# Attention, dense layer and soft mixture of experts in one kernel: the first batch's reduction of v moved behind the first pair's weights, and three loads of w_in moved ahead of five loads of v

## The chip, the core and the metric

The kernel runs on one core of a Trainium2 chip. The metric is the device time of one execution in microseconds. Before the change three executions took 735.56, 733.87 and 732.2 us, a median of 733.87 us. One further execution, 740.27 us long, was profiled; every row below comes from that one.

## What is computed

Three layers follow one another, on 4 batches of 12 heads, 448 positions and 64 columns per head:

```python
scores = scale * np.matmul(q, k.transpose(0, 1, 3, 2))      # masked above the diagonal
attn = softmax(scores);  x = np.matmul(attn, v)             # -> (1792, 768)
h = x @ w_in;  g = np.maximum(0.01 * h, h);  x = g @ w_out  # w_in (768, 2048), float64 in memory
logits = x @ phi                                            # soft mixture of experts, 8 experts of 4 slots
slot_input = softmax(logits, axis=0).T @ x
out = softmax(logits, axis=1) @ (relu(slot_input @ w1) @ w2)
```

## The kernel before, in words

Attention goes pair by pair: 24 pairs of two heads, six to a batch. A pair is written as three slots (`attention_slots`). For pair n they hold, in this order: `attend(n-1)`, the product of the previous pair's weights with its v (PSUM tile O); `lowering(n)`, which transposes the row maxima of pair n on TensorE (mps) and copies them to mr on ScalarE; three calls of `maxima(n+1, ...)`, whose scores (S_3, then S_0 with row blocks 0 and 2, then S_1) VectorE reduces into mxe by the line L361 (junk); three calls of `weights(n, g)` (T_0, T_1, T_2), each ended by an exponential on ScalarE (L397) and, for the last two, by a selection (L401) and sums (L406, L410) on GpSimd; `inverses` and `columns` of the pair before, with a reciprocal on VectorE (L438) and the scaling of O by s_v (L458); and at the end `qk_stacks(n+2)`, four plus four transposes (qkps), with the loads for later pairs behind them.

`reduce_v(n)` takes the largest absolute value of one pair's v on VectorE (L324). With the sixth pair of a batch it also reduces the six numbers (L327) and calls `pow2_scale`, which spreads the result over the partitions by a small matmul (L111, tile v_ps) and works out a power of two from it in five small VectorE instructions (L113 to L121): s_v, used first in `columns`, and inv_v. Before the loop the kernel before calls `reduce_v` for all six pairs of batch 0.

Between the slots, units of w_in are converted from float64: `load_raw` loads a unit of 768 KB (raw_i), ScalarE takes the absolute value (L196) and the sign (L197), VectorE the largest (L199), a shift (L200) and a merge (L201), a small matmul (w_ps) and the same small instructions give the scale (L113 to L121), ScalarE multiplies the sign by it (L215), GpSimd multiplies the two (L216) and splits the product (L220, L223). Six units belong to the first stage, the six pairs of batch 0, with three buffers for the raw data.

The order on each engine is set by a scheduler with the program's order as a start; the matmuls called through `mm` and `tr` keep the order in which they are written (`in_order`), while those called as `nc.tensor.matmul` may be placed by the scheduler. Every load is issued from SyncE (SP) in the order of the code. Once set, each engine carries out its own list strictly in order.

After the first stage the 16 column groups of w_in times x (PSUM tile H) are interleaved with the attention of the next batch, then come the units of w_out, the logits, and in the end the experts, whose weights (w) are loaded while they are used.

Of the kernel before, what the change touches and what calls it, by code (L numbers as in the profile page):

```python
# [29 lines left out]
def as_float(bits):  # L30
    return struct.unpack("<f", struct.pack("<I", bits))[0]
# [3 lines left out]
def tile_attn_moe_softmoe(ctx: ExitStack, tc: tile.TileContext, q, k, v, w_in, w_out, phi, w1, w2, out, dbg=None):  # L35
    nc = tc.nc
# [10 lines left out]
    NP = H // 2  # L47
# [10 lines left out]
    ident = const.tile([128, 128], F32, name="ident")  # L58
# [30 lines left out]
    def ps_tr(name, shape=(128, 512)):  # L89
        return psum.tile(list(shape), F32, tag="tr", bufs=TR[0], name=name)  # L90
# [12 lines left out]
    mm = partial(in_order, nc.tensor.matmul)  # L103
# [3 lines left out]
    def pow2_scale(absmax, name, shift=23, bias=0, out=None):  # L107


        ps = ps_tr(f"{name}_ps", (128, 128))  # L110
        nc.tensor.matmul(ps, absmax.to_broadcast([128, 128]), ident, start=True, stop=True)  # L111
        m1 = const.tile([128, 1], F32, tag="p2_m1", bufs=2, name=f"{name}_m1")
        nc.vector.tensor_reduce(m1, ps, AX.X, ALU.max)  # L113
        nc.vector.tensor_scalar(m1, m1, as_float((27 + bias) << shift), None, ALU.max)
        e = const.tile([128, 1], I32, tag="p2_e", bufs=2, name=f"{name}_e")
        nc.vector.tensor_scalar(e, m1.bitcast(I32), shift, None, ALU.logical_shift_right)
        si = const.tile([128, 2], I32, tag="p2_s" + name[0], bufs=4, name=f"{name}_s")
        nc.vector.tensor_scalar(si[:, 0:1], e, -(2**23), (268 + bias) * 2**23, ALU.mult, ALU.add)
        if out is None:
            out = si[:, 1:2].bitcast(F32)  # L120
        nc.vector.tensor_scalar(out.bitcast(I32), e, 2**23, -(14 + bias) * 2**23, ALU.mult, ALU.add)  # L121
        return si.bitcast(F32)[:, 0:1], out
# [31 lines left out]
    def load_raw():  # L154

        while waiting:
            u = waiting[0]
            kind, f, h, stage = u
            pool, n = pools[stage], BUFS[stage][0]
            if pool is None or sum(x[3] == stage for x in raws) == n:  # L160
                return
            waiting.pop(0)
            w = DM if h is None else DH
            t = pool.tile([128, w, 2], I32, tag="raw", bufs=n, name=f"raw_{kind}{f}_{h}")
            with tc.issue_after(last_load[0]):
                if kind == "i":
                    nc.sync.dma_start(
                        t.rearrange("p (c f) t -> p c (f t)", f=128),
                        w_in32[:, 256 * f : 256 * (f + 1)].rearrange("(c p) f -> p c f", p=128),
                    )  # L170
                else:
                    c0 = 2 * w * (h or 0)
                    nc.sync.dma_start(
                        t.rearrange("p c t -> p (c t)"), w_out32[128 * f : 128 * (f + 1), c0 : c0 + 2 * w]
                    )
            raws[u] = t
# [3 lines left out]
    def loaded_last():  # L180
        last_load[0] = next(
            i for i in reversed(nc.cur_bb.bb.instructions[-80:]) if i.engine == mybir.EngineType.SP
        )
# [112 lines left out]
    def load_qk(n):  # L296
        b, hp = divmod(n, NP)
        t = att.tile([CP, 2, 2 * NI * D], F32, tag="qk", bufs=2, name=f"qk{n}")
        t = t.rearrange("p j (c x) -> p j c x", c=NI)
        for j, src in enumerate((q, k)):  # L300
            for a in range(2):
                nc.sync.dma_start(
                    t[:, j, :, D * a : D * (a + 1)], src[b, 2 * hp + a].rearrange("(c p) d -> p c d", p=CP)
                )
        qk_t[n] = t
        loaded_last()

    def load_v(n):
        b, hp = divmod(n, NP)
        t = vring.tile([CP, 2 * NI, D], F32, tag="v", bufs=VRING, name=f"v{n}")  # L310
        nc.sync.dma_start(t, v[b, 2 * hp : 2 * hp + 2].rearrange("h (j p) d -> p (h j) d", p=CP))
        v_t[n] = t
        loaded_last()
# [4 lines left out]
    def reduce_v(n):  # L318

        b, hp = divmod(n, NP)  # L320
        if hp == 0:
            v_am[b] = am = const.tile([128, NP + 1], F32, tag="v_am", bufs=2, name=f"v_am{b}")
            nc.vector.memset(am, 0.0)
        nc.vector.tensor_reduce(v_am[b][:CP, hp : hp + 1], v_t[n], AX.XY, ALU.max, apply_absolute_value=True)  # L324
        if hp == NP - 1:
            am = v_am[b]
            nc.vector.tensor_reduce(am[:, NP:], am[:, :NP], AX.X, ALU.max)  # L327
            s_v[b], inv_v[b] = pow2_scale(am[:, NP:], f"v{b}")

    def qk_stacks(n):  # L330

        t = qk_t.pop(n)
        st = att.tile([128, 2, 2, S], F32R, tag="qs", bufs=2, name=f"qkt{n}")
        for j in range(2):
            p = ps_tr(f"qkps{n}_{j}", (128, S))
            for c in range(NI):
                tr(p[:, CP * c : CP * (c + 1)], t[:, j, c], ident[:CP, :CP])
            nc.scalar.copy(st[:, j, 0], p)  # L338
            nc.vector.tensor_tensor(st[:, j, 1], p, st[:, j, 0].bitcast(F32), ALU.subtract)  # L339
        st_t[n] = st  # L340

    def maxima(n, tiles):

        st = st_t[n]
        ps = psum.tile([CP, 2, 512], F32, tag="S", bufs=2, name=f"S{n}_{tiles[0]}")
        at = 0
        for i in tiles:
            w = CP * (i + 1)
            for a in range(2):
                r = slice(64 * a, 64 * a + 64)  # L350
                mm(
                    ps[:, a, at : at + w], st[r, 0, 0, CP * i : w], st[r, 1, 0, :w], start=True, stop=True,
                    skip_group_check=True,
                )
            at += w
        at = 0
        for i in tiles:
            w = CP * (i + 1)
            for a in range(2):
                junk = att.tile([CP, S], BF16, tag="junk", bufs=1, name=f"junk{n}_{i}_{a}")  # L360
                nc.vector.tensor_tensor_reduce(  # L361
                    out=junk[:, :w], in0=ps[:, a, at : at + w], in1=mask[:, S - w :], scale=-1.0, scalar=3e38,
                    op0=ALU.add, op1=ALU.min, accum_out=mxe[n % 2][:, 64 * a + i : 64 * a + i + 1],
                )
            at += w
# [126 lines left out]
    def attention_slots():  # L492


        for n in range(2):
            qk_stacks(n)
            load_qk(n + 2)
            if n == 0:
                for tiles in TILES:
                    maxima(0, tiles)  # L500
        for x in range(NP):
            reduce_v(x)
        for n in range(NPAIR + 1):
            here, more = n < NPAIR, n + 1 < NPAIR
            if n > 0:
                attend(n - 1)
            if here:
                lowering(n)
            if more:
                maxima(n + 1, TILES[0])  # L510
            if here:
                weights(n, 0)
            yield
            if n > 0:
                inverses(n - 1)
            if more:
                maxima(n + 1, TILES[1])
            if here:
                weights(n, 1)
            yield  # L520
            if n > 0:
                columns(n - 1)
            if here:
                weights(n, 2)
            if more:
                maxima(n + 1, TILES[2])
            if n + 2 < NPAIR:
                qk_stacks(n + 2)
                if n + 4 < NPAIR:
                    load_qk(n + 4)  # L530
            if n + NP < NPAIR:
                load_v(n + NP)
            if NP <= n + NP - 1 < NPAIR:
                reduce_v(n + NP - 1)
            yield

    TILES = ((3,), (0, 2), (1,))
    slots_of_attention = attention_slots()


# [208 lines left out]
    if True:  # L749
        pools[0] = tc.alloc_tile_pool(name="conv1", bufs=1)  # L750
        load_qk(0)
        load_qk(1)
        for n in range(NP):
            load_v(n)
        load_raw()
        nc.sync.dma_start(phi_sb, phi.rearrange("(c p) s -> p c s", p=128))
        stage(SLOTS * NP + LEAD, EARLY[0])
        tc_release(pools[0])
# [96 lines left out]
        for c in range(4):  # L855
            wo = loaded.pop(("wo", c))
            for h in range(2):
                for t in range(4):
                    nc.tensor.matmul(
                        psi[h][32 * t : 32 * t + 32], gdt[:, t, c], wo[:, t, 384 * h : 384 * (h + 1)],  # L860
                        start=c == 0, stop=c == 3, skip_group_check=True,
# [17 lines left out]
        for e in range(E):  # L879
            ph = ps2(f"ph{e}", (128, 256), tag="h", bufs=4)  # L880
            for hf in range(2):
                wt = loaded.pop(("w1", (e, hf)))
                for t in range(3):
                    for g in range(4):
                        nc.tensor.matmul(  # L885
                            ph[32 * g : 32 * g + 32], sit[:, 3 * hf + t], wt[:, t, 256 * g : 256 * (g + 1)],
                            start=hf == 0 and t == 0, stop=hf == 1 and t == 2, skip_group_check=True,
# [69 lines left out]
        for x, (t0, nt, c0, cols) in enumerate(pieces):  # L957
# [4 lines left out]
            for h in (0, 1) if cols == DM else (c0 // DH,):  # L962
                for t in range(nt):
# [3 lines left out]
                        start=t0 + t < 4, stop=t0 + t >= 8 * E - 4, skip_group_check=True,  # L967
# [52 lines left out]
```

## Time and profile before

| what | value |
|---|---|
| median of three executions | 733.87 us (732.2 to 735.56) |
| profiled execution | 740.27 us, of which 738.5 us are the span of the profile |
| busy share of the span: PE, DVE, ACT, POOL | 87%, 47%, 41%, 31% |
| shares of the chain that ended last: PE, DMA, ACT, DVE, POOL | 59%, 15%, 8%, 7%, 4% |

PE is TensorE, DVE is VectorE, ACT is ScalarE, POOL is GpSimd, SP is SyncE. Times in rows are microseconds from the start of the span. "L324" is line 324 of the kernel. In a timeline row the number in brackets is how long the engine had been idle, and what ended it. Instructions on one engine overlap a little at their ends, so the distance from one start to the next is what an instruction costs in a row of busy ones; it is up to 0.1 us less than the duration shown. The whole change is in the first 45 us of the program, so nearly all rows come from there.

### The profile page before, as it was taken

The page shows a single profiled execution, that of the slowest core. Times are in us where ns is not written, and L with a number is a line of the kernel's source. Part 1 is how long each engine was busy: PE and PEld are TensorE (multiplying, and loading weights), DVE is VectorE, ACT ScalarE, POOL GpSimd, SP SyncE. Part 2 cuts the span into 40 slices and gives each one's busy share as a digit, 9 for nine tenths or more (in the row PEclk, how much of TensorE's full clock was granted, in tenths as well). Part 3 has the DMA queues.
Part 4 walks back from the last instruction along what each step waited for, and adds up shares of the span by engine and source line. Part 5 has one row for each costly group of instructions (what it writes and reads, how often), then busy time and mean ns, then how long its engine had stood idle before and what let it go on. Part 6 is the DMA issues. An engine that isn't in the chain of part 4 may idle for free.

```text
span 738.5 us, 13147 instructions
## 1 busy us (share of the span) xinstructions
PE 639.2 (87%) x5196; PEld 372.0 (50%) x5196; DVE 344.6 (47%) x923; ACT 305.9 (41%) x615; POOL 228.9 (31%) x247
## 2 busy tenths in 40 slices
PE   3888769999898999899999989999999997984573
PEld 2555445555555556566555555664656543541122
DVE  5887655666864544453354544324444433110013
ACT  1777543756774455444345454422322220110013
POOL 4577832656873332441223332320000000000000
PEclk9999968999999999899999999999999999999867
DMA  9933263455544454421153222014859247999988
GB/s 195 249 81 76 62 186 93 122 145 148 152 145 157 124 174 141 136 93 51 51 145 90 66 65 66 22 51 171 300 224 338 87 172 297 409 399 401 392 276 261
DMA packets 117709, 125.73 MB, mean 170 GB/s; under 512 B 69520, under 2 KB 99216, under 8 KB 117648
## 3 DMA queue, kind: packets, MB, share of 16 engines
q1 hardware_dynamic: 117648, 124.90, 52.6%
q8 instruction: 41, 0.67, 0.4%
q14 instruction: 20, 0.16, 0.1%
HBM read 105.74 MB, written 19.14 MB: 169 GB/s over the span
## 4 chain that ended last, share of the span: by engine, by line
PE 59%; DMA 15%; ACT 8%; DVE 7%; POOL 4%; issue 4%; SPq 2%; DVEq 0%; ACTq 0%; POOLq 0%
PE H L100 25%; DMA w<-in_moe_w_dram 7%; PE O L100 7%; PE gps L100 4%; PE T L100 4%; DMA v<-in_v_dram 3%; PE pg L100 2%; PE ph L885 2%; PE L L100 2%; DMA raw_i_None<-in_moe_w_in_dram 2%; PE qkps L100 2%; ACT mr L373 2%; PE dn L100 2%; PE rb L100 2%; DMA raw_o<-in_moe_w_out_dram 2%
## 5 line engine op out<-in xcount | busy, mean ns | idle before, releaser
L100 PE MATMUL H<-x,w 128*128 128x448 f16 x1152 | 244.4, 358 | 6.0 <-DVE g L615 6.0
L100 PEld LDWEIGHTS <-w 128*128 128x128 f16 x1152 | 110.1, 99 | 110.4 <-issue 29.7
L361 DVE CUSTOM_DVE_ANT_0 junk<-S,mask 112x448 bf16<-112x448 f32 (+1 forms) x192 | 84.9, 442 | 36.0 <-PE S L100 32.7
L615 DVE SCALAR_TENSOR_TENSOR g<-H,iv,g 128x448 f32<-128x448 f32 x58 | 39.6, 683 | 98.4 <-ACT g L614 96.0
L614 ACT ACTIVATE g<-H,iv 128x448 f32<-128x448 f32 x58 | 36.6, 631 | 81.2 <-PE H L100 70.9
L397 ACT ACTIVATE P<-T 112x672 f32<-112x672 f32 (+1 forms) x72 | 56.8, 788 | 32.3 <-PE T L100 32.3
L100 PE MATMUL O<-P,v 112*64 112x448 f32 (+3 forms) x384 | 59.2, 453 | 5.8 <-POOL P L401 4.6
L100 PE MATMUL T<-qkt 64*112 64x336 f32 (+3 forms) x576 | 58.7, 315 | 5.2 <-ACT P L397 4.5
L401 POOL TENSOR_SCALAR_AFFINE_SELECT P<-P 112x448 f32<-112x448 f32 x48 | 29.4, 613 | 99.9 <-ACT P L397 99.9
L965 PE MATMUL po<-w,hz 128*32 128x384 f32 x256 | 30.8, 608 | 24.9 <-DMA w<-in_moe_w_dram 24.9
L100 PEld LDWEIGHTS T<-qkt 64*112 64x112 f32 x576 | 44.8, 183 | 11.5 <-ACT P L397 5.8
L100 PEld LDWEIGHTS O<-P,v 112*64 112x64 f32 x384 | 27.9, 151 | 36.6 <-issue 16.9
L373 ACT ACTIVATE mr<-mps,own 128x112 fp32r<-128x112 f32 x96 | 26.1, 355 | 45.4 <-PE mps L100 45.4
L410 POOL TENSOR_TENSOR tsum<-tsum,P 112x448 f32<-112x448 f32 (+1 forms) x48 | 43.9, 915 | 2.7
L406 POOL TENSOR_TENSOR tsum<-P 112x672 f32<-112x672 f32 x24 | 40.7, 1694 | 1.7
L554 ACT COPY g_nat<-gps 112x512 f32<-112x512 f32 x32 | 18.7, 584 | 53.5 <-PE gps L100 53.5
L556 DVE COPY g_nat<-gps 112x512 f32<-112x512 f32 x32 | 22.1, 692 | 37.8 <-PE gps L100 37.5
L460 POOL TENSOR_TENSOR x<-rs,x 128x448 f16<-128x448 f32 x24 | 25.3, 1054 | 46.1 <-ACT x L459 46.1
L339 DVE TENSOR_TENSOR qkt<-qkps,qkt 128x448 fp32r<-128x448 f32 x48 | 28.3, 620 | 21.9 <-ACT qkt L338 21.8
L216 POOL TENSOR_TENSOR cv_i_None<-cv_i_None,cs_i_None 128x768 f32<-128x768 f32 x16 | 26.8, 1682 | 34.1 <-ACT cs_i_None L215 34.0
L100 PE MATMUL S<-qkt 64*112 64x448 f32 (+1 forms) x192 | 33.2, 387 | 3.6 <-DVE mxe L361 2.8
L100 PE MATMUL T<-mr,onesr 64*112 64x448 f32 (+1 forms) x192 | 32.1, 331 | 4.2 <-ACT mr L373 4.2
(178 smaller groups left out, 936.5 us busy)
## 6 DMA issues: line engine op xcount, KB each, us to landing
w<-in_moe_w_dram SPq DMA_DIRECT2D x32, 1536.0 KB, 18.2
raw_i_None<-in_moe_w_in_dram SPq DMA_DIRECT2D x16, 768.0 KB, 6.0
raw_o_None<-in_moe_w_out_dram SPq DMA_DIRECT2D x10, 768.0 KB, 5.1
g_far<-g SPq DMA_DIRECT2D x32, 224.0 KB, 2.0
gb<-g_far SPq DMA_DIRECT2D x8, 896.0 KB, 7.7
wo<-wsc SPq DMA_DIRECT2D x4, 1536.0 KB, 6.8
qk<-in_q_dram SPq DMA_DIRECT2D x48, 112.0 KB, 2.8
qk<-in_k_dram SPq DMA_DIRECT2D x48, 112.0 KB, 2.8
```

The costliest lines, as they stand in the source:

```text
L100: op(*args, **kwargs)
L216: nc.gpsimd.tensor_tensor(t, t, sg, ALU.mult)
L339: nc.vector.tensor_tensor(st[:, j, 1], p, st[:, j, 0].bitcast(F32), ALU.subtract)
L361: nc.vector.tensor_tensor_reduce(out=junk[:, :w], in0=ps[:, a, at : at + w], in1=mask[:, S - w :], scale=-1.0, scalar=3e38, op0=ALU.add, o ...
L373: nc.scalar.activation(mr[:, i], ps, AF.Copy, scale=own[:, i : i + 1])
L397: nc.scalar.activation(x[:, :, o : o + at], ps[:, :, :at], AF.Exp, scale=SCALE)
L401: nc.gpsimd.affine_select(out=d, in_=d, compare_op=ALU.is_ge, fill=0.0, base=0, pattern=[[0, 4], [1, CP]], channel_multiplier=-1,)
L406: nc.gpsimd.tensor_tensor(tsum[:CP], p[0][:CP, :, 0, CP:], p[0][:CP, :, 1, : S - CP], ALU.add)
L410: nc.gpsimd.tensor_tensor(y, y, p[1][:CP, :, j, : S - CP * (j + 2)], ALU.add)
L614: nc.scalar.activation(g, ps, AF.Copy, scale=iv[b][:, 0, f : f + 1])
L615: nc.vector.scalar_tensor_tensor(g, ps, iv[b][:, 1, f : f + 1], g, ALU.mult, ALU.max)
L965: nc.tensor.matmul(po[h][32 * g : 32 * g + 32], hp[:, (t0 + t) % 8], wt[:, t, DH * h - c0 : DH * (h + 1) - c0], start=t0 + t < 4, stop=t0 ...
```

## The change

Three edits. The small matmul of `pow2_scale` for batch 0 goes through `mm`, which binds it to its place in the written order of TensorE. The reductions of v of batch 0 move from ahead of the pair loop into it: pairs 0 to 4 ahead of `attend(0)`, and the sixth, with the power of two, behind `weights(1, 0)`. And the first three units of w_in are asked for behind v of pair 0 and ahead of v of pairs 1 to 5.

```diff
-        nc.tensor.matmul(ps, absmax.to_broadcast([128, 128]), ident, start=True, stop=True)
+        (mm if name == "v0" else nc.tensor.matmul)(ps, absmax.to_broadcast([128, 128]), ident, start=True, stop=True)
@@ attention_slots
-        for x in range(NP):
-            reduce_v(x)
         for n in range(NPAIR + 1):
             here, more = n < NPAIR, n + 1 < NPAIR
+            if n == 1:
+                for x in range(NP - 1):
+                    reduce_v(x)
             if n > 0:
                 attend(n - 1)
...
                 weights(n, 0)
             yield
+            if n == 1:
+                reduce_v(NP - 1)
             if n > 0:
                 inverses(n - 1)
@@ the loads at the start
         load_qk(0)
         load_qk(1)
-        for n in range(NP):
+        load_v(0)
+        load_raw()
+        for n in range(1, NP):
             load_v(n)
-        load_raw()
```

On TensorE, before the change, the matmul v_ps of batch 0's largest v stands between the transposes of q and k of pair 1 (qkps) and the transposed maxima of pair 0 (mps):

```order
L100 MATMUL qkps_1_242<-ident,qk_163 128x112 x4
L111 MATMUL v_ps<-ident,v_am_254 128x128
L100 MATMUL mps_273<-ident,mxe_143 128x112
L100 MATMUL S_3_280<-qkt_234 112x448 x2
L100 MATMUL T_0_287<-qkt_187 112x448 x6
L100 MATMUL T_0_287<-mr_275,onesr 112x448 x2
```

After the change the same place on TensorE reads:

```order
L100 MATMUL qkps_1_242<-ident,qk_163 128x112 x4
L100 MATMUL mps_254<-ident,mxe_143 128x112
L100 MATMUL S_3_261<-qkt_234 112x448 x2
L100 MATMUL T_0_268<-qkt_187 112x448 x6
L111 MATMUL w_ps<-ident,w_am_278 128x128
L100 MATMUL T_0_268<-mr_256,onesr 112x448 x2
```

v_ps is gone from here (it now stands behind T_0 of pair 1), and the matmul w_ps of the first unit of w_in, which stood behind S_0 of pair 1, has moved up into T_0.

On ScalarE the copies (CAST) of the transposed q and k of pair 1 (qkt_234) now have the first unit of w_in between them. This is the place after the change; before it, the two copies stood next to each other:

```order
L338 CAST qkt_234<-qkps_0_235 128x448
L196 ACTIVATE cv_i_None<-raw_i_None 128x768
L197 ACTIVATE cs_i_None<-raw_i_None 128x768
L338 CAST qkt_234<-qkps_1_242 128x448
L373 ACTIVATE mr_256<-mps_254,own 128x112 x4
```

So the second copy, and mr behind it, now stand behind the arrival of the first raw_i.

On VectorE this is the stretch before the change from the first row block of S_0 of pair 1 to the last, whose end lets TensorE start S_1 (junk_0_1 and junk_2_0, junk_2_1 are reductions of S_0):

```order
L361 ISA junk_0_1_314,mxe_144<-S_0_307,mask 112x112
L361 ISA mxe_144 112x1
L114 TENSOR_SCALAR w_m_334<-w_m_334 128x1
L201 SCALAR_TENSOR_TENSOR cv_i_None<-raw_i_None,cv_i_None 128x768
L199 TENSOR_REDUCE w_am_557<-cv_i_None 128x1
L361 ISA junk_2_0_316,mxe_144<-S_0_307,mask 112x336
L361 ISA mxe_144 112x1
L116 TENSOR_SCALAR w_e<-w_m_334 128x1
L200 TENSOR_SCALAR cv_i_None<-cv_i_None 128x768
L361 ISA junk_2_1_318,mxe_144<-S_0_307,mask 112x336
```

After the change the same stretch on VectorE is:

```order
L324 TENSOR_REDUCE v_am_387<-v_178 112x1
L361 ISA junk_0_1_295,mxe_144<-S_0_288,mask 112x112
L361 ISA mxe_144 112x1
L201 SCALAR_TENSOR_TENSOR cv_i_None<-raw_i_None,cv_i_None 128x768
L324 TENSOR_REDUCE v_am_387<-v_180 112x1
L361 ISA junk_2_0_297,mxe_144<-S_0_288,mask 112x336
L361 ISA mxe_144 112x1
L324 TENSOR_REDUCE v_am_387<-v_182 112x1
L324 TENSOR_REDUCE v_am_387<-v_184 112x1
L361 ISA junk_2_1_299,mxe_144<-S_0_288,mask 112x336
```

The reductions of v of pairs 1 to 5 (v_176 to v_184) now lie ahead of junk_2_1, and the merge L201 here is that of the third unit; before, it stood behind junk_2_1. From the second pair on, the lists of TensorE and SyncE are the same as before, and those of the other engines but for a few neighbours that changed places.

## Rows read from the trace of the kernel before

**Rows 1.** Chain of waits, first 125 us: start, length, what.

```profile
14.76 7.48 DMA raw_i_None<-in_moe_w_in_dram
34.83 3.13 DMA v<-in_v_dram
```

**Rows 2.** Timeline of TensorE: start, length, instruction, count, idle before.

```profile
17.73 0.77 PE L111 MATMUL v_ps<-ident,v_am 128*128 128x128 f32 x2 [6.35 <-DVE v_am L327]
18.29 0.39 PE L100 MATMUL mps<-ident,mxe 112*128 112x112 f32 x1
19.12 1.32 PE L100 MATMUL T<-qkt 64*112 64x448 f32 x6
28.63 0.52 PE L100 MATMUL S<-qkt 64*112 64x224 f32 x2
34.72 0.32 PE L100 MATMUL mps<-ident,mxe 112*128 112x112 f32 x1
35.26 0.78 PE L100 MATMUL T<-qkt 64*112 64x448 f32 x6
42.52 0.36 PE L100 MATMUL S<-qkt 64*112 64x224 f32 x2 [0.57 <-DVE mxe L361]
```

**Rows 3.** Timeline of VectorE, the first 30 us.

```profile
12.25 0.62 DVE L339 TENSOR_TENSOR qkt<-qkps,qkt 128x448 fp32r<-128x448 f32 x1
13.21 0.39 DVE L361 CUSTOM_DVE_ANT_0 junk<-S,mask 112x224 bf16<-112x224 f32 x1
...
17.42 0.16 DVE L327 TENSOR_REDUCE v_am<-v_am 128x1 f32<-128x6 f32 x1
17.90 0.69 DVE L324 TENSOR_REDUCE v_am<-v 112x1 f32<-112x512 f32 x1 [0.32 <-DMA v<-in_v_dram]
...
19.37 0.62 DVE L361 CUSTOM_DVE_ANT_0 junk<-S,mask 112x448 bf16<-112x448 f32 x1
...
28.48 0.15 DVE L118 TENSOR_SCALAR w_s<-w_e 128x1 int32<-128x1 int32 x1
28.60 1.82 DVE L201 SCALAR_TENSOR_TENSOR cv_i_None<-raw_i_None,cv_i_None 128x768 int32<-128x768 int32 x1
```

**Rows 4.** DMA, 0 to 40 us: GB/s of each microsecond; then raw_i's landing after issue.

```profile
GB/s 0 20 170 213 178 204 219 253 218 210 214 204 207 209 207 204 220 285 348 352 349 350 348 301 199 217 199 364 310 251 336 149 101 151 179 39 229 221 350 187
DMA to landing us min/median/max: 5.3/6.3/9.1
```

**Rows 5.** Timeline of SyncE: issue of v of pairs 0 and 1.

```profile
4.97 1.09 SPq L311 DMA_DIRECT2D v<-in_v_dram  x2
```

**Rows 6.** Timeline of ScalarE.

```profile
10.67 0.53 ACT L338 CAST qkt<-qkps 128x448 fp32r<-128x448 f32 x1 [3.79 <-PE qkps L100]
19.99 0.91 ACT L196 ACTIVATE cv_i_None<-raw_i_None 128x768 f32<-128x768 f32 x1
```

**Rows 7.** Groups of VectorE, 13.5 to 29 us: busy us, mean ns; idle before, releaser.

```profile
L201 DVE SCALAR_TENSOR_TENSOR cv_i_None<-raw_i_None,cv_i_None 128x768 int32<-128x768 int32 x3 | 3.7, 1245 | 0.0
L324 DVE TENSOR_REDUCE v_am<-v 112x1 f32<-112x512 f32 x5 | 3.4, 685 | 1.4 <-DMA v<-in_v_dram 1.4
L199 DVE TENSOR_REDUCE w_am<-cv_i_None 128x1 f32<-128x768 f32 x3 | 2.8, 949 | 0.3 <-ACT cv_i_None L196 0.3
```

**Rows 8.** Timeline of GpSimd in the same stretch.

```profile
27.77 1.84 POOL L406 TENSOR_TENSOR tsum<-P 112x672 f32<-112x672 f32 x1
29.73 2.19 POOL L216 TENSOR_TENSOR cv_i_None<-cv_i_None,cs_i_None 128x768 f32<-128x768 f32 x1
```

**Rows 9.** Line L216, 0 to 112 us: duration min/median/max in ns.

```profile
L216 POOL TENSOR_TENSOR cv_i_None<-cv_i_None,cs_i_None x6: 1645/1652/2193, 29.7 to 86.3; 128x768 f32<-128x768 f32 x6
```

**Rows 10.** One window: length, busy (x count) by engine, granted clock, DMA, GB/s.

```profile
20.00:25.00 5.00, 2.50 (x14) 1.34 (x12) 4.63 (x11) 4.34 (x6) 0.00 (x0) 1.00 1.17 310
```

**Rows 11.** Chain of waits, second stage: two groups of the same 18 matmuls.

```profile
194.84 5.25 PE H L100 x18
204.18 3.52 PE H L100 x18
```

## The prediction

> **What bounds the kernel now.** The change touches only the first 45 us, so I went from the page to the chain of waits of that stretch. It does not run through TensorE alone: from 14.76 to 22.24 us it is the landing of a unit of w_in, and behind O of pair 0 a landing of v [rows 1], with short pieces of ScalarE, VectorE and TensorE between. The timeline of TensorE shows the one large hole: idle for 6.35 us until 17.73, for the small matmul v_ps, which waited for VectorE to reduce v of all six pairs. The maxima of pair 0 (mps), which do not need v, stood behind it and ran at 18.29 [rows 2], although VectorE had begun their last reduction at 13.21, 0.39 us long [rows 3]. That wait is what the change takes out. Two marks serve below: S_1 of pair 1 at 28.63 and mps of pair 1 at 34.72 [rows 2], 6.09 us apart, filled by the transposes of pair 2 and O of pair 0.
>
> From the second pair on each pair is a ring: TensorE frees v's buffer, the next v is loaded (3.13 us [rows 1]), VectorE reduces it, then come the reciprocal and TensorE again. Nothing in that ring hangs on a fixed time, so what is won or lost by the end of pair 1 is kept to the end, if the later stages run as before.
>
> **When the first unit of w_in lands.** VectorE now has the first unit's L199 between the maxima of pair 0, and on ScalarE the copy of pair 1's k stands behind its L196 and L197. In front of the unit in the queue lie q and k of pairs 0 and 1 and v of pair 0, 8 x 112 + 224 KB = 1.147 MB. By the GB/s of each microsecond these have passed at 7.6 us (1.004 MB by 7.0, then 0.57 us at 253). The unit is 0.786 MB; where only such units ran the rate was 350 [rows 4], so 2.25 us and its last byte at 9.8. From last byte to landing: the old order's second unit ends with byte 4.55 MB, passed at 21.2, and landed at 22.24 [rows 1], so 1.05. Landing: 10.9. The order of SyncE lets it be issued at 5.5, behind the first of the two issues of v that began at 4.97 [rows 5]; the old units took 5.3 to 9.1 us from issue to landing [rows 4], so the bounds are 10.8 and 14.6. I take 10.9, near the lower end, because the queue in front of it is the shorter one that I could count.
>
> ScalarE finishes the copy that began at 10.67 at 11.2, so L196 (0.91 [rows 6]) is not held up and ends at 12.1. VectorE has L199 from 12.2 on, the last reduction of S_1 from 13.1, and mps runs at 13.5 instead of 18.29: **4.8 us earlier.**
>
> **What comes back in front of S_1.** From there on VectorE has no time to spare, and S_1 of pair 1 must wait until it has gone through the last block of S_0. Before, it took from 13.21 to 28.6 for that, 15.4 us, of which 1.4 idle for v and 0.3 for ScalarE [rows 7]: 13.7 of work. The change moves behind the mark what ran from L327 at 17.42 to 19.37 but for the wait of 0.32 in it (L327, v of pair 6, the small instructions for s_v): 1.6. It moves in front of the mark v of pair 1 (0.685 [rows 7], less an overlap of 0.08: 0.6), the second subtraction of pair 1, which ran at 12.25 (0.62 less the same: 0.5 [rows 3]), and the third unit's merge L201 (0.9): together 2.0. That makes 14.1 us from 12.2, and S_1 at 26.3; four of the old reductions of v were spread by waits and now overlap by 0.08 each, so 26.0. What it needs is there: by the same sum of bytes the second and third unit land at 15.4 and 17.7, and v of pair 5 at 23.5, each at least 0.4 us before VectorE asks.
>
> One term is added. L201 reads two tensors in SBUF. The one at 28.60 took 1.82 us [rows 3] where the other two of its group took 0.95 ((3 x 1.245 - 1.82) / 2 [rows 7]); it ended 0.81 behind the end of L406 on GpSimd at 29.61, and L216, begun at 29.73, took 2.19 [rows 8] instead of 1.65 [rows 9]. So the two took turns, and whoever came second waited for the end of the other. In the new order L216 starts 1.25 us behind L118 (28.48 to 29.73, by way of L215), and L201 stands some 1.37 behind L118, with L121, L200, one v and one block between. If L216 is first, L201 waits until 2.90 and comes out 1.4 us later; if not, nothing. An order that hangs on 0.12 us I cannot tell, so I take half, 0.7, and keep both ends. S_1 then stands at 26.8, **1.8 us earlier** (0.5 to 2.6 with both ends and a landing some 0.6 late): three of the 4.8 us are gone, since VectorE and not TensorE is the bound.
>
> The Trainium skill, Advanced Engine Details and Errata, section VectorE Performance Modes, says that VectorE's second SBUF port is shared with GpSimd and that instructions of the two which use it interfere or block each other. The trace agrees (1.82 us for 0.95 [rows 3, 7]). Taken as slowing both rather than as taking turns, it would cost 0.9 us here whoever came first, and S_1 would stand at 26.9.
>
> **What comes back in pair 1.** mps follows S_1 by the same 6.1 us: GpSimd's selection for O's second half is some four microseconds early and not the bound. Up to S_1 of pair 2, at 42.52 before [rows 2], VectorE's list then changes in three ways. One v moves from in front of the reciprocal to behind the merge, nothing in the sum. The instructions for s_v come in, 0.4. L458, which stood behind the last block, now stands in front of it, 0.6, of which 0.1 was a pause anyway. v_ps adds 0.4 us to TensorE, beside VectorE. **0.9 us lost.**
>
> **The clock in the head.** Six matmuls of T took 1.32 us at 19.12 and 0.78 us at 35.26 [rows 2]: by these durations TensorE ran at the lower of its two levels (1.2 GHz) up to pair 1, though the granted clock is given as 1.00 between 20 and 25 us [rows 10]. It rose while TensorE was busy without a long hole, by mps of pair 1. In the new order a hole of some 2 us opens in front of S_1, so the rise may come a microsecond behind mps. Then S_3 and the first of T take some 0.3 us more. **0.3 us lost**, 0 to 1.
>
> **Sum.** 1.8 - 0.9 - 0.3 = 0.6 us faster. The profiled execution, 740.27 us, would be 739.7. It lies 6.4 us above the median of the three; the change is counted in microseconds of the head, so I take the same 0.6 from the median of 733.87: **733.3 us.**
>
> **Rivals.**
> *The wait saved is kept.* If VectorE has more room than I count, the 4.8 us of mps go through S_1, less 0.9 in pair 1: 730.0. For it: VectorE was idle 1.7 us of the old stretch. Against it: 14 us of work from 12.2 on do not fit in front of 24. Chance 0.17.
>
> *The first unit lands late; slower than before.* Its place is ScalarE's list and VectorE's: the copy of pair 1's k, mr, and the last maximum all stand behind it. Past 10.9 each microsecond moves the rest by one, so from 11.5 on nothing is gained, and at the upper bound of 14.6 the loss is 3.7 - 0.6 = 3.1: 737.0. For it: the old units took up to 9.1 us. Against it: the bytes in front of it are few and the rate in rows 4 is steady. Chance 0.10.
>
> *The later clock decides.* In the second stage 18 matmuls of H took 5.25 us at one place and 3.52 at another [rows 11]; there are three such slow groups in the chain. If a shift of the head changes their number, each is 1.7 us either way; two make 729.9 or 736.7. Against it: the ring shifts as a whole, and with it the pauses in front of them. Chance 0.14.
>
> **Numbers.** The forecast has 0.59, with a range of its own of 731.7 to 735.8 (S_1 0.5 to 2.6 earlier, clock 0 to 1, and 0.5 us of scatter). About 0.5%, 3.7 us, is what a measurement of this kernel can tell from no change. Faster by more: somewhat over half of the first rival (0.10), a quarter of the third (0.04), 0.03 of the forecast: 0.17. Slower by more: 0.04 of the second, 0.04 of the third, 0.01 of the forecast: 0.09. The rest, 0.74, is no change. The range reaches into the rivals on both sides: 730.0 to 736.6.
>
> **What would show it.** In the new trace the hole of 6.35 us in front of v_ps is gone and mps stands near 13.5; the first unit's L196 starts near 11.2; TensorE has a hole of about 2 us in front of S_1 of pair 1, released by VectorE's reduction (L361), with VectorE busy from 12 to 27; S_1 stands near 26.8, mps of pair 1 near 32.9, S_1 of pair 2 near 41.7; from there on each mark is 0.6 to 0.9 us early to the end. I am wrong if S_1 stands before 25 or behind 28.6, if the first L196 starts beyond 11.8, or if the offset of the two traces changes between 45 us and the last loads.

## The result: 1% slower, and the profile after

| | before | after |
|---|---|---|
| time, median | 732.95 us (732.2 to 735.56, 5 runs) | 740.3 us (739.73 to 746.6, 5 runs) |
| ratio, 95% interval | | 1.010 (1.0064 to 1.0137) |
| profiled execution / its span | 740.27 / 738.5 us | 746.6 / 744.8 us |

The kernel became slower by 7.35 us, where 0.6 us less was forecast and the range ended at 736.6. (The median of before is now that of five executions; the forecast started from the 733.87 of three.) The two profiled executions lie 7.3 and 6.3 us above their medians, so they are compared with each other: they differ by 6.3 us.

The quickest reading is one mark per pair. The lag of mps, its start after less its start before, runs over the program like this: -3.7 us at pair 0, -0.35 at pair 1, +1.4 at pair 2, +1.0 to +1.7 up to 137 us, +2.8 to +3.0 from 157 to 378, +2.1 at pairs 20 and 21, +0.9 at pair 22 (446.8), +6.8 at pair 23 (469.8), and 6.3 at the end. So there are two places to look at: the head, and 23 us in the second half that no part of the diff names. (A smaller step, 1.1 us, lies between 137 and 157.)

The head, on TensorE (start, length, instruction, count, idle before; the marks of [rows 2]):

```profile
14.60 0.42 PE L100 MATMUL mps<-ident,mxe 112*128 112x112 f32 x1 [3.44 <-DVE mxe L361]
...
28.30 0.53 PE L100 MATMUL S<-qkt 64*112 64x224 f32 x2 [2.81 <-DVE mxe L361]
30.44 4.00 PE L100 MATMUL O<-P,v 112*64 112x448 f32 x16
34.37 0.31 PE L100 MATMUL mps<-ident,mxe 112*128 112x112 f32 x1
...
42.65 0.36 PE L100 MATMUL S<-qkt 64*112 64x224 f32 x2 [1.55 <-ACT P L397]
43.85 3.36 PE L100 MATMUL O<-P,v 112*64 112x448 f32 x16
47.15 0.45 PE L100 MATMUL mps<-ident,mxe 112*128 112x112 f32 x1
```

The same product O of pair 1 before:

```profile
43.73 2.11 PE L100 MATMUL O<-P,v 112*64 112x448 f32 x16
```

The hole of 6.35 us is gone, and a hole of 2.81 stands in front of S_1 of pair 1, released by VectorE: as forecast in kind. S_1 is 0.33 us early and not 1.8. Two terms made the difference. The timelines of ScalarE, GpSimd and VectorE show them, and the DMA row answers to [rows 4]:

```profile
12.27 0.89 ACT L196 ACTIVATE cv_i_None<-raw_i_None 128x768 f32<-128x768 f32 x1 [1.29 <-DMA raw_i_None<-in_moe_w_in_dram]
23.15 1.64 POOL L216 TENSOR_TENSOR cv_i_None<-cv_i_None,cs_i_None 128x768 f32<-128x768 f32 x1 [13.64 <-ACT cs_i_None L215]
23.26 2.35 DVE L201 SCALAR_TENSOR_TENSOR cv_i_None<-raw_i_None,cv_i_None 128x768 int32<-128x768 int32 x1
```

And DMA in GB/s, one figure for each microsecond from 0 to 40:

```profile
GB/s 0 23 185 184 216 214 216 234 311 331 256 185 162 239 326 379 361 284 191 193 186 191 197 195 209 199 184 183 249 341 381 354 267 239 65 54 232 197 307 214
```

The first unit landed just before L196 began at 12.27, some 1.35 us later than the forecast 10.9, and L196 itself began 1.1 us later than forecast (11.2). And L201 met GpSimd's L216 head on: L216 began 0.11 us earlier, and L201 took 2.35 us, 1.4 more than 0.95.

Why the unit was late stands in the packets. A unit of 768 KB is 768 packets of 1 KB, and those of q, k and v are under 512 B. From 10 to 11 us and from 11 to 12 us the queue moved:

```profile
DMA packets 875, 0.26 MB, mean 256 GB/s; under 512 B 823, under 2 KB 875, under 8 KB 875
DMA packets 723, 0.18 MB, mean 185 GB/s; under 512 B 714, under 2 KB 723, under 8 KB 723
```

So the last 52 + 9 packets of the unit went out among those of q and k of pair 2, which were asked for behind it, the last one at 11.4 us. The landing came some 0.85 us behind that.

The second place, 447 to 457 us. First before, ScalarE and then TensorE:

```profile
447.28 1.09 ACT L373 ACTIVATE mr<-mps,own 128x112 fp32r<-128x112 f32 x4 [2.35 <-PE mps L100]
449.29 0.55 ACT L197 ACTIVATE cs_o<-raw_o 128x384 bf16<-128x384 f32 x1 [0.93 <-DMA raw_o<-in_moe_w_out_dram]
```

```profile
443.56 3.30 PE L100 MATMUL O<-P,v 112*64 112x448 f32 x16
448.41 0.46 PE L100 MATMUL T<-mr,onesr 64*112 64x448 f32 x2
448.80 1.88 PE L100 MATMUL H<-x,w 128*128 128x448 f16 x9
450.51 0.60 PE L100 MATMUL gps<-ident,g 128*112 128x128 f32 x4
```

And after:

```profile
451.43 0.54 ACT L197 ACTIVATE cs_o<-raw_o 128x384 bf16<-128x384 f32 x1 [4.45 <-DMA raw_o<-in_moe_w_out_dram]
451.88 1.07 ACT L373 ACTIVATE mr<-mps,own 128x112 fp32r<-128x112 f32 x4
```

```profile
445.61 2.11 PE L100 MATMUL O<-P,v 112*64 112x448 f32 x16
447.65 0.32 PE L100 MATMUL mps<-ident,mxe 112*128 112x112 f32 x1
447.90 0.46 PE L100 MATMUL S<-qkt 64*112 64x448 f32 x2
448.19 0.77 PE L100 MATMUL T<-qkt 64*112 64x448 f32 x6
453.00 0.71 PE L100 MATMUL T<-mr,onesr 64*112 64x448 f32 x2 [4.04 <-ACT mr L373]
453.65 3.54 PE L100 MATMUL H<-x,w 128*128 128x448 f16 x9
456.98 0.89 PE L100 MATMUL gps<-ident,g 128*112 128x128 f32 x4
```

Two instructions of ScalarE have changed places. Before, the four copies that make mr of pair 22 came first, and the sign (L197) of the first half of w_out unit 15 waited for its load behind them; TensorE had no hole there. After, the sign stands in front. Its load was asked for at 448.11 and the sign ran 3.3 us later, at 451.43; before it was 3.24 (446.05 to 449.29), so the load is no slower. But mr, ready to be copied since mps at 447.65, waited behind the sign, and TensorE stood for 4.04 us. Then nine matmuls of H took 3.54 us for 1.88: TensorE came out of the hole at the lower level (1.2 GHz). Over these nine the granted clock is 0.50 after (453.6 to 457.2) and 1.00 before (448.8 to 450.7). 4.04 + 1.66 of H + 0.25 of T = 5.95, and the lag grew by 5.9 (0.86 to 6.76).

Not all of that is the exchange's. Before, too, the granted clock was 0.50 for a while here, from 444.3 to 447.7, just ahead of the mark, and O of pair 21 took 3.30 us; after, it was still at 1.00 there and O took 2.11. That is why the lag had shrunk from 2.05 at pair 21 to 0.86 at pair 22. From pair 21 to pair 23, over both stretches, it grew by 4.7 us. On ScalarE neighbours changed places at two more points behind the head, at 53 to 55 and at 106 us, and no step of a microsecond stands there (lag +1.4 to +1.6 and +1.0 to +1.6).

The order of ScalarE's instructions at this place, before and then after:

```
L373 ACTIVATE mr22_5100<-mps22_5098,own_124 128x112 x4
L197 ACTIVATE cs_o15_0_5339<-raw_o15_0_5161 128x384
L397 ACTIVATE P0_448_145<-T22_0_5112 112x2x448
```

```
L197 ACTIVATE cs_o15_0_5339<-raw_o15_0_5161 128x384
L373 ACTIVATE mr22_5100<-mps22_5098,own_124 128x112 x4
```

### The profile page after: what moved, and what is told of

Same layout as the page of the kernel before. It is cut to its first block, busy times and chain, and to the rows that moved or that the text cites. A ratio compares the mean times of both kernels' runs of the same rounds, so it can differ in the third digit from the quotient of the medians.

```text
span 744.8 us, 13144 instructions
## 1 busy us (share of the span) xinstructions
PE 639.9 (86%) x5196; PEld 372.7 (50%) x5196; DVE 345.1 (46%) x923; ACT 305.8 (41%) x615; POOL 228.4 (31%) x247
## 4 chain that ended last, share of the span: by engine, by line
PE 58%; DMA 14%; DVE 9%; ACT 8%; POOL 4%; issue 4%; SPq 1%; DVEq 0%; ACTq 0%; POOLq 0%
PE H L100 25%; DMA w<-in_moe_w_dram 7%; PE O L100 6%; PE gps L100 4%; PE T L100 3%; DMA v<-in_v_dram 3%; PE pg L100 2%; PE ph L889 2%; PE L L100 2%; DMA raw_o<-in_moe_w_out_dram 2%; DMA raw_i_None<-in_moe_w_in_dram 2%; DVE cv_i_None L201 2%; PE dn L100 2%; PE rb L100 2%; ACT mr L373 2%
## 5 line engine op out<-in xcount | busy, mean ns | idle before, releaser
L216 POOL TENSOR_TENSOR cv_i_None<-cv_i_None,cs_i_None 128x768 f32<-128x768 f32 x16 | 26.3, 1647 | 48.8 <-ACT cs_i_None L215 48.8
```

The costliest lines, as they stand in the source:

```text
L216: nc.gpsimd.tensor_tensor(t, t, sg, ALU.mult)
```

## The experiments

Theory: most of the loss is this one exchange, and the rest is VectorE's work in pairs 0 and 1. Rivals: the new order of the loads costs by itself; or the reductions alone cost. The first four ran on one chip, where the kernel before had a median of 735.08 us (28 runs, 731.76 to 741.84); for the last two it was 734.12 (17 runs). The profile of the kernel before, 740.27 us, lies 5 to 6 us above these medians, so the lag of another profile against it shows where a step is, and its end says little of the medians.

**The exchange undone.** The changed kernel; the sign stands behind the copies to mr again, and nothing else in the order differs.

```diff
-        nc.scalar.activation(sg, hw.bitcast(F32), AF.Sign)
+        with tc.issue_after(mr_last[0]) if (kind, f, h) == HELD else ExitStack():   # HELD = ("o", 15, 0)
+            nc.scalar.activation(sg, hw.bitcast(F32), AF.Sign)
```

> The changed kernel with one thing put back: on ScalarE the sign (L197) of the first half of w_out's unit 15 stands behind the four copies to mr of pair 22, as in the kernel before, instead of in front of them. Theory A, that this exchange of two neighbours some 400 us behind the edits makes most of the loss (mr waited 4.4 us for a load of w_out): 735 to 736 us, 4.4 to 5.6 us less than the changed kernel's 740.3, and no such wait at 451. Rival B, that the head and the clock make the loss and the wait would only move to the next user of that load: 739.5 to 740.5.

Measured: 737.54 us, 1.0034 (1.0008 to 1.0061). ScalarE, then TensorE, in its profile:

```profile
449.42 1.09 ACT L379 ACTIVATE mr<-mps,own 128x112 fp32r<-128x112 f32 x4 [2.09 <-PE mps L100]
451.70 0.55 ACT L198 ACTIVATE cs_o<-raw_o 128x384 bf16<-128x384 f32 x1 [1.19 <-DMA raw_o<-in_moe_w_out_dram]
```

```profile
450.68 0.37 PE L100 MATMUL T<-mr,onesr 64*112 64x448 f32 x2
450.98 1.88 PE L100 MATMUL H<-x,w 128*128 128x448 f16 x9
```

The sign ran at about the same time as in the changed kernel (451.70 and 451.43), but now nobody waited: no hole, H at 1.88. The lag stays at +2.1 to +2.5 us from 200 to 470 us with no step. Of 1.0% two thirds are gone (1.0 - 0.34 = 0.66%, 4.9 us), and the two intervals do not touch. By the ratio that is what theory A expected (735 to 736 against 732.95); the microseconds lie above because this chip's median of before is 2.1 us higher.

**The exchange alone.** The kernel before, with mr of pair 22 placed behind that sign (a few neighbours in the output's tail changed as well).

```diff
+        if (kind, f, h) == ("o", 15, 0):
+            for i in mr_22:
+                tc.add_manual_dep(i, sign.name, ...)    # order only
```

> The kernel before with that exchange alone: the copies to mr of pair 22 stand behind the sign of w_out's unit 15. Head and loads are as before. Theory A: 4.4 to 5.6 us slower than the kernel before, 737.4 to 738.6, with mr waiting some 3 to 4 us for raw_o. Rival B: within 1 us of the kernel before, 732 to 734.

Measured: 739.31 us, 1.0059 (1.0033 to 1.0084): 4.3 us (2.4 to 6.2) for two neighbours that changed places, with the diff's own edits left out; theory A expected 4.4 to 5.6, rival B less than 1. The output's tail shows no loss in the profile (lag +0.2 at pair 23, -2.0 at the end). ScalarE and TensorE:

```profile
447.05 0.54 ACT L197 ACTIVATE cs_o<-raw_o 128x384 bf16<-128x384 f32 x1 [4.36 <-DMA raw_o<-in_moe_w_out_dram]
447.49 1.07 ACT L381 ACTIVATE mr<-mps,own 128x112 fp32r<-128x112 f32 x4
```

```profile
448.62 0.46 PE L100 MATMUL T<-mr,onesr 64*112 64x448 f32 x2 [1.52 <-ACT mr L381]
```

The idle ScalarE is there. In this one execution TensorE's hole was 1.52 us, and the granted clock was 0.50 ahead of it (439.7 to 446.5) and 1.00 behind it. So its profile shows less than the ten runs do: the lag grew by 2.8 us from pair 21 to pair 23, 1.7 of them from pair 22.

**The loads alone** (third edit; mr in front of the sign).

> Only the third edit: three units of w_in loaded ahead of five pairs' v, while all reductions of v stay ahead of the pair loop. v of pair 5 then lands near 24 and v_ps, which still stands in front of mps, near 25 instead of 17.7. If the wait for v is what rules the head: S_1 of pair 1 some 5 us later and 737 to 740 us. If the head is ruled by VectorE's total work, as the changed kernel suggests, the reductions fill the wait and it is 2 to 4 us: 735 to 737. pair 22's mr stands in front of the sign here, so theory A adds nothing.

Measured: 740.22 us, 1.0072 (1.0044 to 1.01). With v reduced at the old place, all of v must come in behind the units before TensorE goes on:

```profile
25.03 0.77 PE L111 MATMUL v_ps<-ident,v_am 128*128 128x128 f32 x2 [13.89 <-DVE v_am L327]
```

mps of pair 0 is 7.3 us late and pairs 1 to 6 some 5.5, as the first of the two expectations had it (the wait for v rules the head). Then the lag melts to 2.4 at 117 us, 1.6 at 240 and 0.3 at 425. This does not show that a late head is caught up: between pairs 6 and 7, where 3.2 us go, the granted clock was 0.82 here and 0.58 in the profile of before. The median is 5.3 us over before's, about the lag of pairs 1 to 6; how much of a late head is kept stays open. So this rival is no small thing: the new order of the loads costs by itself as much as the exchange does. But that price is v_ps waiting for all of v, and in the changed kernel v_ps stands behind T_0 of pair 1.

**The reductions alone** (first two edits; loads in the old order, mr in front of the sign).

> Only the first two edits: the reductions of v of batch 0 behind the first pair's weights, loads in the old order. VectorE and ScalarE do not meet a unit of w_in before pair 0's maxima, so mps of pair 0 near 13.5 and S_1 of pair 1 some 3 us earlier than before. pair 22's mr stands in front of the sign. Theory A (the head's gain is kept, the loss of the changed kernel lies at 450 us): 729 to 732. Rival B (a shift of the head costs more in later clock than it gives): 733 to 737.

Measured: 736.4 us, 1.0006 (0.9974 to 1.0038), so theory A's gain did not come. mps of pair 0 came 4.5 us early and of pair 1 6.6; then pair 2 was 1.5 late. VectorE, GpSimd, ScalarE and TensorE show the eight microseconds:

```profile
35.30 4.17 DVE L201 SCALAR_TENSOR_TENSOR cv_i_None<-raw_i_None,cv_i_None 128x768 int32<-128x768 int32 x1
...
39.65 0.14 DVE L121 TENSOR_SCALAR v_s<-v_e 128x1 int32<-128x1 int32 x1
```

```profile
35.41 1.65 POOL L223 TENSOR_TENSOR w<-cv_i_None,w 128x768 f16<-128x768 f32 x1
37.02 1.64 POOL L216 TENSOR_TENSOR cv_i_None<-cv_i_None,cs_i_None 128x768 f32<-128x768 f32 x1
38.61 2.32 POOL L406 TENSOR_TENSOR tsum<-P 112x672 f32<-112x672 f32 x1
```

```profile
39.82 0.48 ACT L585 ACTIVATE iv<-inv_w,v_s 128x1 f32<-128x1 f32 x2 [3.12 <-DVE v_s L121]
40.44 0.71 ACT L397 ACTIVATE P<-T 112x672 f32<-112x672 f32 x1
```

```profile
41.20 0.53 PE L100 MATMUL S<-qkt 64*112 64x224 f32 x2 [4.62 <-ACT P L397]
43.34 4.00 PE L100 MATMUL O<-P,v 112*64 112x448 f32 x16
```

L201 stretched over two whole operations of GpSimd and ended 0.8 us behind the second (the third, begun in between, took 2.32 us, where 1.6 is usual: 1.61 and 1.62 in the next run's profile); v_s stood behind it, ScalarE's iv behind v_s, the exponential that frees the scores behind iv, and S_1 of pair 2 behind that, after a hole of 4.62 us. Behind the hole the granted clock was 0.50 (43.3 to 47.3), and O took 4.00 us for the 2.11 of before. So the loss is this wait and the clock that followed it.

**The reductions of v put off.** The first experiment, and the reductions of v 1 to 5 held behind the readings of S_0 of pair 1.

```diff
-                for x in range(NP - 1):
-                    reduce_v(x)
+                with tc.issue_after(s0_last[0]):
+                    for x in range(NP - 1):
+                        reduce_v(x)
```

> The changed kernel with the sign of w_out unit 15 behind the copies to mr (as in the run with that sign held back), and the five reductions of batch 0's v (5 x 0.67 us on VectorE) held behind the readings of the first block of scores of pair 1, so that S_1 of pair 1 no longer waits for them. Theory (VectorE's work sets pair 1, and what is won is kept): S_1 of pair 1 at about 25.5 instead of 28.3 us, mps of pair 1 at about 31.5 instead of 34.5, mps of pair 2 at about 44.7 instead of 47.7, and 0.996 to 1.000 of the kernel before, against 1.0034 for the run with the sign alone held. Rival (VectorE's work is only put off; pair 2 then waits for it, as it did where the reductions alone were moved): mps of pair 1 at 31 to 32 but mps of pair 2 again at 47 or later, and 1.002 to 1.005.

Measured: 732.86 us, 0.9995 (0.9968 to 1.0022). TensorE:

```profile
12.59 0.42 PE L100 MATMUL mps<-ident,mxe 112*128 112x112 f32 x1 [1.54 <-DVE mxe L362]
...
24.69 0.48 PE L100 MATMUL S<-qkt 64*112 64x224 f32 x2
25.10 1.76 PE L100 MATMUL qkps<-ident,qk 112*128 112x112 f32 x8
26.79 3.42 PE L100 MATMUL O<-P,v 112*64 112x448 f32 x16
30.14 0.31 PE L100 MATMUL mps<-ident,mxe 112*128 112x112 f32 x1
```

S_1 stands without a hole and the five reductions run beside S_1, qkps and O. mps of pair 1 is 4.35 us earlier than in the first experiment (34.49). From mps of pair 0 to mps of pair 1 it takes 17.55 us, against 19.21 there (15.28 to 34.49). The other 2.7 are a second change: the edit let the scheduler put the last reduction of pair 0's maxima ahead of the first unit's L199 (12.06 and 13.51 us; 14.75 and 13.88 in the first experiment), so that mps of pair 0 no longer waits for a load. Part of that was lost again at once: S_3 of pair 1 stood for ScalarE until 14.72 (15.63 in the first experiment). From S_3 to mps of pair 1 it is 3.4 us less here; 1.4 of these are the merge L201 (0.95 us for 2.34), which leaves some 2 for the reductions. The profile keeps the lead to the end (mps -4.6 at pair 1, -4.5 at 157 us, -8.3 at 470), but the median is that of the kernel before. The interval of 0.9995 just meets the 1.0034 of the first experiment's (they share 1.0008 to 1.0022), so that the rest of the loss sits in VectorE's list of pairs 0 and 1 is likely, not proved.

**The turn-taking merge taken out of the fourth.** The reductions alone, with that L201 held behind the last reading of the scores of pair 2.

```diff
+            tc.add_manual_dep(pair["merge"], pair["junk"].name, ...)    # order only
```

> The kernel before with the first two edits alone (loads in the old order), and the merge of w_in unit 3 on VectorE (L201, which took 4.17 us beside two GpSimd operations at 35.3 us in the run with these edits alone) held behind the last reading of the scores of pair 2. Theory (that one turn-taking merge made pair 1 lose what pair 0 had won): the copy of v_s stands at about 35.4 instead of 39.6, S_1 of pair 2 comes at 37 to 38 instead of 41.2, mps of pair 2 at about 43 instead of 47.3 (before: 45.8), and 0.993 to 0.997 of the kernel before. Rival (pair 1 is set by the sum of the work on VectorE and ScalarE, not by this one): mps of pair 2 stays at 46 to 47.5, 1.000 or above. Whatever the first pairs do, the order of many later neighbours changes with this edit (reciprocal, exp, signs), so a loss of some us in the middle of the program is possible: it would show as a step in the offset of mps between two pairs, as the one at 450 us in the changed kernel.

Measured: 743.06 us, 1.0121 (1.0079 to 1.0164). Its local point held: v_s at 34.78, mps of pair 2 at 41.51 instead of 47.28. The time did not follow. From pair 2 to pair 3 the lead of 4.3 us turned into a lag of 1.7: TensorE waited for the reciprocal (first row below; the second is a wait for GpSimd a pair later), and from 48.1 to 58.3 us its granted clock was 0.50. The lag went on to +6.1 at pair 5 and was -0.6 at pair 7. At 447 us came the known step, +4.3 us (lag -0.5 to +3.8): moving one merge had exchanged sign and mr again. The median is 8.9 us over before's; the step is about half of that, and where the rest goes is open. TensorE at both waits, then ScalarE:

```profile
48.67 1.76 PE L100 MATMUL rb<-r,first 128*64 128x112 f32 x16 [1.96 <-DVE r L450]
71.69 1.16 PE L100 MATMUL O<-P,v 112*64 112x224 f32 x8 [2.75 <-POOL P L413]
```

```profile
448.97 0.54 ACT L197 ACTIVATE cs_o<-raw_o 128x384 bf16<-128x384 f32 x1 [4.44 <-DMA raw_o<-in_moe_w_out_dram]
449.41 1.07 ACT L385 ACTIVATE mr<-mps,own 128x112 fp32r<-128x112 f32 x4
```

So the exchange stood in three kernels with quite different heads, and each profile has a step there: 4.7, 2.8 and 4.2 us from pair 21 to pair 23, against -0.2, 1.3, -0.1 and 0.2 in the four other runs. No version tried beats the kernel before.

## Why the prediction was wrong

**The step that failed:** "Nothing in that ring hangs on a fixed time, so what is won or lost by the end of pair 1 is kept to the end, if the later stages run as before." They did not run as before. The scheduler had exchanged two neighbours on ScalarE 400 us behind the edits, and that exchange is 4.9 us by its removal and 4.3 by itself, of 7.35. (The rest lies in the sizes of the head's terms below: with the exchange undone 0.34%, 2.5 us, are left, and at pair 2 the lag was already +1.4 us.) It stood in the two orders side by side, to be read before any run. And before's rows price it: a sign that cannot start before 449.29, ahead of copies that began at 447.28, delays them by 449.29 + 0.45 - 447.28 = 2.5 us, and a group of H at the lower clock is 1.7 more. That is 4.2 us, and I took them for neighbours without a price. (That it meets the measured 4.3 so closely is partly luck: in the three profiles the hole was 4.04, 1.52 and 2.50 us, and the clock fell with two of them.)

**The hole in front of v_ps goes, mps at 13.5.** Right in kind; 14.60, so 3.7 us early and not 4.8. The term that was off is the landing, 12.25 for 10.9. The count took the unit's bytes as one block behind q, k and v. By the sum of the GB/s row that block ends at 10.1 (forecast 9.8), but 61 of its packets went out behind that among those of q and k of pair 2, the last at 11.4. From the last packet to the landing it took 0.85 us, near the 1.05 taken. The landing is within the stated bounds (10.8 to 14.6), but L196 at 12.27 is beyond the 11.8 that I had set as a sign of being wrong. The three other runs with this order of the loads have L196 at 11.60, 12.59 and 12.95.

**S_1 is bound by VectorE, 1.8 early.** Right in kind, the size off: 0.33. The difference is the late unit (1.1) and the full turn-taking, 1.4 where half of it, 0.7, was taken: 26.8 + 1.1 + 0.7 = 28.6, measured 28.30. The Trainium skill, Advanced Engine Details and Errata, section VectorE Performance Modes, has instructions of VectorE and GpSimd that use the shared port interfere or block each other; the runs show blocking: the L201 of 1.82, of 2.35 and of 4.17 us each ended 0.8 us behind the end of a GpSimd operation.

**mps follows S_1 by 6.1.** Right: 6.07.

**0.9 lost in pair 1.** S_1 to S_1 takes 14.35 us, 13.89 before: 0.5 lost. But VectorE's list, from which the term was added up, is not what released S_1 of pair 2: that was an exponential on ScalarE (hole of 1.55 us). The size came out near by luck.

**0.3 for the clock in the head.** Nothing was lost by pair 1: the six matmuls of T behind its mps took 0.77 us, 0.78 before. A fall came a pair later: behind the hole of 1.55 us in front of S_1 of pair 2 (granted clock 0.61 from 43.8 to 47.2, 1.00 before) O took 3.36 us, against 2.11 before. So 1.25 us, just over the bound of 1, and the lag at pair 2 is +1.4 where -0.8 was expected.

**The rivals.** "The wait saved is kept" fell: 3.4 of 3.7 us were gone by S_1. "The first unit lands late" happened in part: 1.35 of the 3.7 us to its bound. "The later clock decides" had the right price, 1.7 us for a group of H, but as a follower: the clock fell in the hole that the exchange made. No rival had a queue on ScalarE with a waiting instruction at its head.

**The signs of being wrong** did their work. S_1 stayed inside its bounds (28.30, with 28.6 the later one), but L196 came beyond 11.8, and the offset of the two traces did change between 45 us and the last loads, 1.1 us at 137 to 157 (the v of a pair landed late: the reduction waits 1.35 us for it, 0.20 before) and 5.9 at 447, of which 4.7 are left over the whole stretch from pair 21 to pair 23.

## What to carry to other kernels

An edit at the head of a scheduled program edits the whole program: compare the two orders to the last instruction, and for each exchange on an in-order engine ask whether the one that moved up waits for a load and whether the one that moved down feeds the bound. A first estimate of the price is in the old trace: the old start of the one that waits, plus its length, less the old start of the other, and the clock of what follows the hole. And where one engine's list fills a stretch, removing a wait in front of it wins little: of 3.7 us won at mps of pair 0, 0.33 were left at S_1.

## What the runs showed of the hardware

A merge on VectorE with both operands in SBUF (L201, 0.95 us alone) took 1.82, 2.35 and 4.17 us, each time ending 0.8 us behind the end of a GpSimd operation on SBUF tensors; the last stretched over two whole operations, though these are separate instructions, and came in ahead of the third. Nor is the delay always VectorE's: in the run with v put off, L201 came 0.05 us ahead of L216 and took 0.95, and L216 took 2.42 for 1.65:

```profile
22.51 0.95 DVE L202 SCALAR_TENSOR_TENSOR cv_i_None<-raw_i_None,cv_i_None 128x768 int32<-128x768 int32 x1
22.56 2.42 POOL L217 TENSOR_TENSOR cv_i_None<-cv_i_None,cs_i_None 128x768 f32<-128x768 f32 x1 [13.05 <-ACT cs_i_None L216]
```

(The lines there are one higher.) A unit of 768 KB does not pass the queue as one block: 61 of its 768 packets went out between 10 and 12 us among some 1500 smaller ones that were asked for behind it. And the time of one execution says little here: on one chip the kernel before ran between 731.76 and 741.84 us, so a step of two traces at one place was worth more than the difference of their ends. Such a step needs the granted clock of both traces beside it, as the 5.9 and 4.7 us at 447 show.
